# Fused attention and expert kernel: row parts earlier in the routing list, five loads of v in the opening, pieces no longer held behind a score tile

## The chip, the cores and the metric

The kernel runs on one core of one Trainium2 chip. The metric is the device time of one execution in microseconds (us): the median over several runs, lower is better. One further execution was recorded by the profiler; its rows are the ones read below. Times inside it count from the start of its span.

## The reference

```python
def _attn_ref(u, v, z):                      # batch 8, seq 2496, d_model 256, d_qk 64
    scores = (1.0 / S) * np.matmul(z, z.transpose(0, 2, 1))
    attn = np.maximum(scores, 0.0) ** 2
    return u * np.matmul(attn, v)

def _moe_ref(x, expert_emb, tau, w1, w2):    # x is the attention's output, 19968 tokens, 8 experts, F = 1024
    logits = normalised(x) @ normalised(expert_emb).T / tau
    expert_idx = np.argmax(logits, axis=1)
    gate_w = softmax(logits) at expert_idx
    out[mask of e] = gate_w * (np.maximum(x[mask] @ w1[e], 0.0) @ w2[e])
```

Each token goes to one expert; the row that is sent to it is the token's attention output.

## The kernel before, in words

**Attention.** The 8 batches are worked through one after the other. A batch b has 5 query groups g of 512 tokens (the last has 448), and a group has 20 steps q, one for each key tile s of 128 tokens. The loop over the 800 (b, g, q, s) makes one step at a time. A score tile exists once for two groups: for a key tile of the group itself or of a later group it is computed by `scores` (two matmuls, L259 and L260), brought to `a` by ScalarE (ReLU L263, square L264) and cut by VectorE in `parts` into a high half (L299) and a low half (L300), two float16 numbers whose sum is the value. They lie in a tile `hl`, of which there are five in turn. Where the key tile is of a later group, the tile is also turned by a DMA transpose on the SP queue (L313 into `tt`, L315 where half of it goes into the tile `joint`), so that the later group need not compute it: the first group of a batch, (b,0), has 16 such transposes, (b,1) fewer, (b,4) none. `scores` runs LOOK = 3 tiles ahead of use. `values` then multiplies the halves with the halves of v (L357, L359, L361) and sums over the 20 steps in the banks `acc`.

**Routing.** When a group's last step is done, `route` gives a list of small pieces, and one piece is popped in each step of the next group, behind `values`. In turn they are: `gate_x` (attention times u, L407), `fold` (for the last group only does it do anything), four `square` (L418, sums of squares on ScalarE), `root` (from L682), `scale` (L426 to L435, which makes `up`, the power of two that brings each row into range), four `split` (a block of 128 tokens each: the high half on ScalarE L441, the low half on VectorE L442, then a transpose of the row on the SP queue, L445, into `rowt`), `logits` (L453 on TensorE, from `rowt`), `norms` (L457 to L459, reads the logits from a bank of `acc` that the group after next will use), `top`, `exps` (L480), `gates`, `rank` (L497, L498 on TensorE), `place` (L507 to L515) and `scatters` (L521, on GpSimd). The route of (b,4) so runs during (b+1,0), and that of (b,0) during (b,1). The index in the list sets the step: piece 0 is popped at once at the end of the group, piece i behind step i-1 of the next group.

**Order of the instructions.** Each engine and each DMA queue works in order. The order is made by a scheduler from the program; `tc.issue_after(x)` keeps what is written under it behind the instruction x on the engine. In this kernel `state["at"]` is the newest ReLU of a score tile on ScalarE (L263), and `state["dv"]` the newest high half on VectorE (L299); every popped piece is issued under both.

**What shares the SP queue.** The loads of v for the next batch (L107, 256 KB each), the pieces of z for its largest value (`scan`, L114), u (L375), the experts' weights (L558, L561) and their stores (L621), and all the transposes, L313, L315 and L445.

**Opening.** z and v are scaled by powers of two that come from their largest absolute values. For batch 0 z is loaded in two pieces, one on the SP queue and one on ScalarE's, then v in ten loads of two key tiles that alternate between the two queues; `scan_max` (L121) reduces each of the twelve pieces on VectorE. ScalarE then splits z (L192, L194) with VectorE (L195, L199), and v (L223, with L224 on VectorE).

**Experts.** From about 1360 us on, TensorE multiplies the sorted rows with the experts' weights, to the end. The change does not touch this part.

## Time and profile before

| | us |
|---|---|
| median of 3 runs | 2193.96 (2192.53 to 2197.41) |
| the profiled execution | 2197.87 |
| its span | 2196.1 |
| busy TensorE (PE) | 2106.9, 96% of the span |
| busy VectorE (DVE) | 1333.8, 61% |
| busy ScalarE (ACT) | 1014.2, 46% |
| busy GpSimd (POOL) | 334.0, 15% |

The table gives each engine's busy time over the whole span, an average over the attention, where all engines work, and the experts, where TensorE works almost alone. The profile's strip of TensorE's granted clock shows 8 or 9 tenths of full speed in the first slice and 9 in all others, where 9 stands for anything from 90% up, so short stretches at half speed must be looked for by windows. In the strip of DMA activity the attention's slices stand at 6 to 9 tenths of the 16 DMA engines' time. An idle stretch of an engine counts only where a chain of waits to the end goes through it.

### The profile page before, as it was taken

To read this page: it belongs to the slowest core of one execution; us is meant where nothing else is said; L and a number is where in the kernel's file an instruction comes from. 1 tells how busy PE (TensorE), PEld (TensorE's weight loads), DVE (VectorE), ACT (ScalarE), POOL (GpSimd) and SP (SyncE) were. 2 spreads that over 40 slices of the span, in tenths; PEclk is the share of its full clock that TensorE was granted. 3 is DMA by queue.
4 is the path that set the end of the run, shared out by engine and by line. 5 is a ranking of instruction groups with operands and counts; after the bars stand their busy time and mean duration, and the time that the engine had idled before them with its cause. 6 is when DMAs were issued, how large, how long until landed. Compare 5 with 4: busy or idle time off the path is not lost.

```text
span 2196.1 us, 50747 instructions
## 1 busy us (share of the span) xinstructions
PE 2106.9 (96%) x19210; PEld 1794.6 (82%) x19210; DVE 1333.8 (61%) x4009; ACT 1014.2 (46%) x2131; POOL 334.0 (15%) x344
## 2 busy tenths in 40 slices
PE   5999899899899899999999999999999999999998
PEld 3788688688688688788788788888888888888888
DVE  7887777777787777787777765533333333333333
ACT  6666566566566566566566653222222222222211
POOL 0011022011011011011011011211211121111111
PEclk8999999999999999999999999999999999999999
DMA  6977977977967966976977787533333342247574
GB/s 172 176 145 170 198 142 171 194 141 166 201 140 163 206 141 153 205 153 152 201 156 154 146 162 181 132 88 88 72 75 88 88 89 58 50 109 201 133 211 115
DMA packets 661769, 317.61 MB, mean 145 GB/s; under 512 B 562949, under 2 KB 639246, under 8 KB 655376
## 3 DMA queue, kind: packets, MB, share of 16 engines
q1 hardware_dynamic: 644688, 271.39, 59.5%
q0 software_dynamic: 15184, 41.24, 6.2%
q8 instruction: 152, 2.49, 0.5%
q10 hardware_dynamic: 1648, 1.70, 0.3%
q14 instruction: 97, 0.79, 0.1%
HBM read 255.11 MB, written 59.60 MB: 143 GB/s over the span
## 4 chain that ended last, share of the span: by engine, by line
PE 83%; DMA 7%; DVE 6%; issue 1%; ACT 1%; SPq 1%; DVEq 0%; ACTq 0%; POOL 0%; POOLq 0%
PE acc L357 12%; PE acc L361 12%; PE acc L359 12%; PE po L974 6%; PE po L973 6%; PE po L975 6%; PE sc L259 4%; PE sc L260 3%; DMA rowt<-row 2%; PE acc L364 1%; PE acc L366 1%; PE pt L453 1%; DVE smxv L121 1%; DMA scan<-in_zT_dram 0%; DMA zt<-in_zT_dram 0%
## 5 line engine op out<-in xcount | busy, mean ns | idle before, releaser
L263 ACT ACTIVATE a<-sc 128x512 f32<-128x512 f32 (+1 forms) x480 | 270.6, 564 | 410.6 <-PE sc L260 347.6
L521 POOL DMA_INDIRECT xs<-row,dsti x160 | 173.7, 1086 | 1063.2 <-issue 286.9
L264 ACT ACTIVATE a<-a 128x512 f32<-128x512 f32 (+1 forms) x480 | 285.0, 594 | 7.8
L357 PE MATMUL acc<-vv,tt 128*128 128x256 f16 x1152 | 268.8, 272 | 0.0
L359 PE MATMUL acc<-vv,tt 128*128 128x256 f16 x1152 | 268.8, 272 | 0.0
L980 POOL DMA_INDIRECT out_dram<-ot,me x159 | 154.6, 972 | 660.0 <-DVE ot L979 626.9
L973 PE MATMUL po<-w,hh 128*128 128x256 f16 x928 | 253.0, 273 | 0.0
L974 PE MATMUL po<-w,hh 128*128 128x256 f16 x928 | 252.9, 273 | 0.0
L975 PE MATMUL po<-w,hl 128*128 128x256 f16 x928 | 252.9, 273 | 0.0
L979 DVE TENSOR_SCALAR ot<-po,me,w 128x256 f32<-128x256 f32 x116 | 58.3, 540 | 216.4 <-PE po L975 215.1
L259 PE MATMUL sc<-z 128*128 128x512 f16 (+1 forms) x480 | 178.7, 372 | 5.1 <-DVE z L199 3.5
L260 PE MATMUL sc<-z,z 128*128 128x512 f16 (+1 forms) x480 | 178.7, 372 | 0.0
L361 PE MATMUL acc<-vv,tt 128*128 128x256 f16 x1152 | 178.0, 273 | 0.0
L975 PEld LDWEIGHTS <-hl 128*128 128x128 f16 x1272 | 124.5, 98 | 14.4
L974 PEld LDWEIGHTS <-hh 128*128 128x128 f16 x1272 | 124.5, 98 | 14.3
L973 PEld LDWEIGHTS <-hh 128*128 128x128 f16 x1272 | 124.5, 98 | 14.2
L361 PEld LDWEIGHTS <-tt 128*128 128x128 f16 x1152 | 112.7, 98 | 13.0
L359 PEld LDWEIGHTS <-tt 128*128 128x128 f16 x1152 | 112.6, 98 | 12.8
L357 PEld LDWEIGHTS <-tt 128*128 128x128 f16 x1152 | 112.5, 98 | 12.8
L973 PE MATMUL po<-wb,hh 128*128 128x256 f16 x344 | 93.8, 273 | 0.0
L974 PE MATMUL po<-wb,hh 128*128 128x256 f16 x344 | 93.8, 273 | 0.0
L975 PE MATMUL po<-wb,hl 128*128 128x256 f16 x344 | 93.8, 273 | 0.0
(5238 smaller groups left out, 5504.2 us busy)
## 6 DMA issues: line engine op xcount, KB each, us to landing
w<-wsd SPq DMA_DIRECT2D x64, 1026.0 KB
wa<-wsd SPq DMA_DIRECT2D x46, 1024.0 KB
w<-wsd SPq DMA_DIRECT2D x42, 1024.0 KB
wb<-wsd SPq DMA_DIRECT2D x24, 1026.0 KB
vr<-in_v_dram SPq DMA_DIRECT2D x75, 256.0 KB
ut<-in_u_dram SPq DMA_DIRECT2D x72, 256.0 KB
wr<-in_w_dram SPq DMA_DIRECT2D x64, 256.0 KB
wsd<-wo SPq DMA_DIRECT2D x64, 256.0 KB
```

What stands on the lines that cost most here:

```text
L259: nc.tensor.matmul(sc[:, :n], z1[:, ss], z1[:, t0:t0 + n], start=True, stop=False)
L260: nc.tensor.matmul(sc[:, :n], z1[:, ss], z2[:, t0:t0 + n], start=False, stop=True)
L263: state["at"] = nc.scalar.activation(a[:, :n], sc[:, :n], AF.Relu, scale=2.0 ** -SHIFT).ins
L264: nc.scalar.activation(a[:, :n], a[:, :n], AF.Square)
L357: nc.tensor.matmul(outs[j], piece(ph, j), vh, start=first and j % 2 == 0, stop=False, skip_group_check=True)
L359: nc.tensor.matmul(outs[j], piece(ph, j), vl, start=False, stop=False, skip_group_check=True)
L361: nc.tensor.matmul(outs[j], piece(pl, j), vl if last else vh, start=False, stop=ends, skip_group_check=True)
L521: put = nc.gpsimd.indirect_dma_start(xs[:, :], bass.IndirectOffsetOnAxis(ap=loc["dsti"][:m, j:j + 1], axis=0), row[:m, j, :], None)
L973: nc.tensor.matmul(o, hh[:, f, t], wh, start=(f == 0), stop=False)
L974: nc.tensor.matmul(o, hh[:, f, t], wl, start=False, stop=False)
L975: nc.tensor.matmul(o, hl[:, f, t], wh, start=False, stop=(f == NF - 1))
L980: put = nc.gpsimd.indirect_dma_start(out, bass.IndirectOffsetOnAxis(ap=me.bitcast(U32)[:, j, 1:2], axis=0), ot[:, j, :], None, bounds_chec ...
```

## The change

Three edits.

1. In `route` the list is rearranged: `gate_x` moves from index 1 to 0, the four squares from one per step into two pairs (indices 2 and 3), `root` from 7 to 5, `scale` from 8 to 6, the splits from 9 to 12 to 7 to 10. The list is padded so that `logits` and all behind it stand one index later than before (18 instead of 17).
2. A popped piece is no longer held behind the newest score tile's instructions (`state["at"]`, `state["dv"]`).
3. In the opening z comes for its largest value in three pieces (512, 512 and 256 columns; SP, ACT, SP) in buffers of the ring of v, and v in five loads of four key tiles (512 KB), all on the SP queue, into buffers that the experts' weights use later (`v_first`). `scan_max` has 3 + 5 pieces instead of 2 + 10.

```diff
--- before.py
+++ after.py
@@ -116,7 +116,7 @@
 
     def scan_max(b, what, i):
         if i == 0:
-            n = NVP if what == "v" else ZSCANS if b else 2
+            n = (NVP if b else NV0) if what == "v" else ZSCANS if b else 3
             scan[b, what] = sml.tile([P, n], F32, name="smx" + what)
         nc.vector.tensor_reduce(scan[b, what][:, i:i + 1], scan.pop((b, what, i)), axis=AX.X, op=ALU.max,
                                 apply_absolute_value=True)
@@ -203,6 +203,26 @@
         c = slice(c0, c1)
         nc.sync.dma_start(z1[DQ:P, c], z2[0:DQ, c])
         nc.sync.dma_start(z2[DQ:P, c], z1[0:DQ, c])
+
+    VC = 4
+    NV0 = ceil_div(NST, VC)
+    v0 = []
+
+    def v_first(i):
+
+        if not v0:
+            assert NST * D <= 3 * min(W1, W2)
+            v0.extend([wp.tile([P, W1], F32, name="v0a", tag="wr1"), wp.tile([P, W2], F32, name="v0b", tag="wr2"),
+                       wp.tile([P, 2 * max(W1, W2)], F16, name="v0c", tag="wo").bitcast(F32)])
+        per = min(W1, W2) // D
+        assert per % VC == 0
+        q = i * VC
+        n = min(VC, NST - q)
+        t = v0[q // per][:, q % per * D:(q % per + n) * D].rearrange("p (j d) -> p j d", d=D)
+        nc.sync.dma_start(t, v[0, q * P:(q + n) * P, :].rearrange("(j p) d -> p j d", p=P))
+        for j in range(n):
+            vraw[0, q + j] = t[:, j, :]
+        scan[0, "v", i] = t.rearrange("p j d -> p (j d)")
 
     def v_split(b, s):
         vt = vraw.pop((b, s))
@@ -539,9 +559,9 @@
         assert nj == 4
         none = lambda: None
         one = lambda f, *a: lambda: f(*a)
-        begin = [none, gate_x, none, both(fold, one(square, 0)), one(square, 1), one(square, 2), one(square, 3), root, scale]
-        begin += [one(split, j) for j in range(nj)]
-        begin += [none] * (NST - 3 - len(begin))
+        two = lambda j: both(one(square, j), one(square, j + 1))
+        begin = [gate_x, none, both(fold, two(0)), two(2), none, root, scale] + [one(split, j) for j in range(nj)]
+        begin += [none] * (NST - 2 - len(begin))
         return begin + [logits, norms, top, exps, gates, none, none, rank, none, place, scatters]
 
 
@@ -639,21 +659,22 @@
     nc.vector.memset(ones_f, 1.0)
     first = tc.manual_schedule(engines={mybir.EngineType.DVE, mybir.EngineType.Activation})
     first.__enter__()
-    z0 = wp.tile([P, W1], F32, name="z0", tag="wr1")
-    for i in range(2):
-        t = z0[:, 2 * i * SCAN:2 * (i + 1) * SCAN]
-        src = zT[0, i * (DQ // 2):(i + 1) * (DQ // 2), :]
-        (nc.scalar if i % 2 else nc.sync).dma_start(t, src.rearrange("a c -> (a c)").rearrange("(p w) -> p w", p=P))
-        scan[0, "z", i] = t
+    zw = SP * DQ // P
+    zsrc = zT[0, 0:DQ, :].rearrange("a c -> (a c)").rearrange("(p w) -> p w", p=P)
+    for i in range(3):
+        c = slice(512 * i, min(512 * (i + 1), zw))
+        zs = vring.tile([P, 2, D], F32, name="zs", tag="vv").rearrange("p j d -> p (j d)")[:, :c.stop - c.start]
+        (nc.scalar if i == 1 else nc.sync).dma_start(zs, zsrc[:, c])
+        scan[0, "z", i] = zs
     nc.scalar.dma_start(idt, ident)
     z_tiles(0)
     ZN = ceil_div(SP, ZC)
     for k in range(2):
         z_load(0, k * ZC)
-    for i in range(NVP):
-        scan_load(0, "v", i, nc.scalar if i % 2 else nc.sync)
+    for i in range(NV0):
+        v_first(i)
     z_load(0, 2 * ZC)
-    for i in range(2):
+    for i in range(3):
         scan_max(0, "z", i)
     for f in scale_pieces(0, "z"):
         f()
@@ -664,9 +685,9 @@
     halves = {}
     for i in range(LOOK + 1):
         probs[direct[i]] = scores(*direct[i])
-    for i in range(NVP):
+    for i in range(NV0):
         scan_max(0, "v", i)
-        if i == NVP - 3:
+        if i == NV0 - 2:
             halves[direct[0]] = parts(*direct[0], probs.pop(direct[0]))
     z_load(0, 3 * ZC)
     for f in scale_pieces(0, "v"):
@@ -1110,8 +1131,7 @@
                     todo.pop(0)[2]()
         values(accs[b, g], b, g, q, s, *half(b, g, s))
         if queue:
-            with tc.issue_after(state["at"]), tc.issue_after(state["dv"]):
-                queue.pop(0)()
+            queue.pop(0)()
         if i >= wnext and not state["pm"]:
             wnext += wgap
             if wq:
```

Lines of the program behind `v_first` stand 20 further down in the changed kernel: L313 becomes L333, L445 becomes L465, and so on.

What the order of the instructions becomes, at three places.

**The SP queue in the middle of group (2,0)**, where the route of (1,4) runs. `tt<-hl` are the transposes of score tiles, `rowt` those of the row blocks, `vr`, `wsd`, `wr1`, `scan` plain loads and stores. Before:

```order
L107 DMA vr_5785<-in_v_dram 128x2x256
L621 DMA wsd_73<-wo_5348 128x2x512
L313 DMA_TRANSPOSE tt_5806<-hl__5803 128x8x128
L445 DMA_TRANSPOSE rowt_5801<-row1_100 128x4x128
L313 DMA_TRANSPOSE tt_5806<-hl__5829 128x8x128
L445 DMA_TRANSPOSE rowt_5801<-row1_100 128x4x128
L313 DMA_TRANSPOSE tt_5806<-hl__5854 128x8x128
L445 DMA_TRANSPOSE rowt_5801<-row1_100 128x4x128
L107 DMA vr_5865<-in_v_dram 128x2x256
L558 DMA wr1_5882<-in_w1_dram 128x512
L445 DMA_TRANSPOSE rowt_5801<-row1_100 128x4x128
L313 DMA_TRANSPOSE tt_5806<-hl__5885 128x8x128
```

and now:

```order
L333 DMA_TRANSPOSE tt_5667<-hl__5769 128x8x128
L107 DMA vr_5779<-in_v_dram 128x2x256
L641 DMA wsd_73<-wo_5335 128x2x512
L465 DMA_TRANSPOSE rowt_5738<-row1_100 128x4x128
L333 DMA_TRANSPOSE tt_5799<-hl__5796 128x8x128
L465 DMA_TRANSPOSE rowt_5738<-row1_100 128x4x128
L333 DMA_TRANSPOSE tt_5799<-hl__5822 128x8x128
L333 DMA_TRANSPOSE tt_5799<-hl__5844 128x8x128
L107 DMA vr_5855<-in_v_dram 128x2x256
L578 DMA wr1_5869<-in_w1_dram 128x512
L333 DMA_TRANSPOSE tt_5799<-hl__5872 128x8x128
L114 DMA scan_5882<-in_zT_dram 128x320
```

The score tile of `hl__5854` before is that of `hl__5844` now (and `hl__5885` that of `hl__5872`). Of the four row transposes two now stand above the rows shown, so all four are ahead of that tile's transpose, where two were; the plain loads keep their place beside the score transposes.

**ScalarE early in group (2,1)**, where the route of (2,0) runs. `a<-sc` (ReLU) and `a<-a` (square) are the two instructions of a score tile, `sq` the squares of the routing, `row` its splits, and `ex` the exponentials of the route before. Before:

```order
L263 ACTIVATE a_6190<-sc_6187 128x512
L418 ACTIVATE sq_6212,n2_6102<-x_6100 128x256
L264 ACTIVATE a_6190<-a_6190 128x512
L263 ACTIVATE a_6222<-sc_6219 128x512
L418 ACTIVATE sq_6241,n2_6102<-x_6100 128x256
L264 ACTIVATE a_6222<-a_6222 128x512
L263 ACTIVATE a_6252<-sc_6249 128x512
L264 ACTIVATE a_6252<-a_6252 128x512
L263 ACTIVATE a_6303<-sc_6300 128x512
L264 ACTIVATE a_6303<-a_6303 128x512
L263 ACTIVATE a_6336<-sc_6333 128x512
L441 ACTIVATE row0_99<-x_6100,up_6321 128x256
```

and now:

```order
L500 ACTIVATE ex_6088<-sh_6077 128x32
L283 ACTIVATE a_6060<-sc_6057 128x512
L284 ACTIVATE a_6060<-a_6060 128x512
L438 ACTIVATE sq_6132,n2_6087<-x_6085 128x256
L438 ACTIVATE sq_6134,n2_6087<-x_6085 128x256
L438 ACTIVATE sq_6152,n2_6087<-x_6085 128x256
L438 ACTIVATE sq_6154,n2_6087<-x_6085 128x256
L461 ACTIVATE row0_99<-x_6085,up_6254 128x256 x4
L283 ACTIVATE a_6181<-sc_6178 128x512
L284 ACTIVATE a_6181<-a_6181 128x512
```

The four squares and the four splits stand together ahead of one score tile; before, the last two squares and the four splits stood between the tiles, at most one for each.

**ScalarE in the opening**, up to its first score tile. Before:

```order
L646 DMA z_110<-in_zT_dram 128x640
L648 DMA idt<-in_ident_dram 128x128
L107 DMA vr<-in_v_dram 128x2x256 x5
L192 ACT_TABLE_LOAD
L192 ACTIVATE z_114<-zt,scz 64x256
L194 ACTIVATE z_115<-zt,scz 64x256
L192 ACTIVATE z_114<-zt,scz 64x256
L194 ACTIVATE z_115<-zt,scz 64x256
L192 ACTIVATE z_114<-zt,scz 64x256
L194 ACTIVATE z_115<-zt,scz 64x256
L263 ACTIVATE a<-sc 128x512
```

and now:

```order
L667 DMA zs<-in_zT_dram 128x512
L669 DMA idt<-in_ident_dram 128x128
L192 ACT_TABLE_LOAD
L192 ACTIVATE z_117<-zt,scz 64x256
L194 ACTIVATE z_118<-zt,scz 64x256
L192 ACTIVATE z_117<-zt,scz 64x256
L194 ACTIVATE z_118<-zt,scz 64x256
L283 ACTIVATE a<-sc 128x512
L284 ACTIVATE a<-a 128x512
```

The five loads of v are gone from ScalarE's queue ahead of the table load, and the first score tile stands ahead of the third pair of z's splits.

## Rows read from the trace of the kernel before

**Rows 1.** Waits of PE over the whole span: total us, times, longest us.

```profile
PE pt L453 <- DMA rowt<-row: 48.2, 22, 3.8
```

**Rows 2.** Stretches: us, busy of each engine, granted PE clock, DMA share, GB/s.

```profile
160.00:1120.00 960.00, 913.36 (x8014) 748.05 (x8012) 728.43 (x2451) 582.79 (x1285) 131.73 (x127) 0.98 0.82 170
365.00:406.00 41.00, 35.88 (x296) 28.07 (x295) 28.72 (x84) 23.34 (x50) 4.14 (x4) 0.92 1.00 211
```

**Rows 3.** Timeline of PE in group (2,0): start, us, engine, operation, idle before.

```profile
387.99 0.35 PE L453 MATMUL pt<-e,rowt 128*128 128x16 f16 x8
391.11 0.28 PE L453 MATMUL pt<-e,rowt 128*128 128x16 f16 x4 [2.77 <-DMA rowt<-row]
393.59 0.27 PE L453 MATMUL pt<-e,rowt 128*128 128x16 f16 x4 [2.21 <-DMA rowt<-row]
...
394.52 1.06 PE L357 MATMUL acc<-vv,hl__5980 128*128 128x256 f16 x4
...
397.08 0.42 PE L357 MATMUL acc<-vv,joint 128*128 128x256 f16 x1
```

**Rows 4.** Timeline of the SP queue in groups (2,0) and (2,1).

```profile
366.85 1.27 SPq L313 DMA_TRANSPOSE tt<-hl__5622  x1
...
384.13 1.23 SPq L445 DMA_TRANSPOSE rowt<-row  x1
385.45 1.27 SPq L313 DMA_TRANSPOSE tt<-hl__5854  x1
...
393.03 0.58 SPq L114 DMA_DIRECT2D scan<-in_zT_dram  x1
...
407.45 1.23 SPq L313 DMA_TRANSPOSE tt<-hl__6214  x1
```

**Rows 5.** Timeline of DVE in group (2,0).

```profile
380.60 0.48 DVE L442 SCALAR_TENSOR_TENSOR row<-x,up,row 128x256 f16<-128x256 f32 x1
...
388.85 0.43 DVE L299 CAST hl__5980<-a 128x512 f16<-128x512 f32 x1 [1.51 <-DMA tt<-hl__5854]
...
395.85 0.49 DVE L121 TENSOR_REDUCE smxz<-scan 128x1 f32<-128x320 f32 x1 [5.63 <-DMA scan<-in_zT_dram]
396.25 0.42 DVE L300 TENSOR_TENSOR joint<-a,joint 128x256 f16<-128x256 f32 x1
```

**Rows 6.** Timeline of all engines in group (2,1), tile by tile.

```profile
403.55 0.42 ACT L418 ACTIVATE sq<-x 128x256 bf16<-128x256 f32 x1 [2.96 <-DVE x L407]
...
407.99 0.43 DVE L299 CAST hl__6245<-a 128x512 f16<-128x512 f32 x1
...
411.47 0.27 PE L357 MATMUL acc<-vv,hl__6245 128*128 128x256 f16 x1
...
413.91 0.50 ACT L441 ACTIVATE row<-x,up 128x256 f16<-128x256 f32 x1
...
425.85 1.30 SPq L313 DMA_TRANSPOSE tt<-hl__6411  x1
...
429.29 0.43 DVE L299 CAST hl__6529<-a 128x512 f16<-128x512 f32 x1 [3.33 <-DMA tt<-hl__6411]
...
431.28 0.26 PE L453 MATMUL pt<-e,rowt 128*128 128x16 f16 x4 [2.80 <-DMA rowt<-row]
...
431.82 1.02 PE L357 MATMUL acc<-vv,hl__6529 128*128 128x256 f16 x4
```

**Rows 7.** Timeline of ACT, DVE and PE in the opening.

```profile
8.11 1.28 ACT L192 ACT_TABLE_LOAD   x1 [8.11 <-DMA vr<-in_v_dram]
...
14.70 0.51 ACT L192 ACTIVATE z<-zt,scz 64x256 f16<-64x256 f32 x1 [3.20 <-DMA zt<-in_zT_dram]
...
18.41 0.43 DVE L299 CAST hl__201<-a 128x512 f16<-128x512 f32 x1 [1.52 <-ACT a L264]
...
21.56 0.16 DVE L132 TENSOR_REDUCE smv<-smxv 128x1 f32<-128x10 f32 x1
...
25.81 0.37 PE L357 MATMUL acc<-vv,hl__201 128*128 128x256 f16 x1 [0.97 <-ACT vv L223]
```

## The prediction

> **What bounds the kernel now.** I read the waits of TensorE (PE) first, then the granted clock by windows, then the timelines around the largest wait, then the opening. One wait stands far above the rest: the routing's logits (L453) wait for the transposed row blocks `rowt`, 48.2 us in 22 waits, none over 3.8 [rows 1]. They lie in 15 groups: the eight (b,1), which host the route of (b,0), and the seven (b,0) from b = 1 on, which host that of (b-1,4). The clock shows a second loss: over the 960 us of the attention's middle the mean granted clock is 0.98, so about 2% or 19 us of full speed is missing at most, and in the 41 us of group (2,0) it is 0.92, so 3.3 us [rows 2]; of TensorE's two levels, 1.2 and 2.4 GHz, this is the lower one for some 6.6 us, behind waits of together 5.0 us [rows 3].
>
> Why are the blocks late? The low half of the last block was made on VectorE at 380.60 [rows 5], but PE got the last `rowt` only at 393.59 [rows 3]. Between lies the SP queue. In (2,0) it is without a real gap from 366.85 to the transposes and loads that end shortly before 407.45, each transpose holding it 1.23 to 1.27 us, and two blocks stand behind score transposes and loads [rows 4]. The DMA engines' share in that window is 1.00 [rows 2]. So the group is bound by what this one queue issues, and PE feels it at the logits first. A second thing is just as tight: the ring of five `hl` tiles. VectorE's high half at 388.85 had waited 1.51 us for the score transpose issued at 385.45 [rows 4, 5], and in (2,1) the one at 429.29 waited 3.33 for that of 425.85, while PE wanted this very tile at 431.82, right behind the logits' wait of 2.80 [rows 6].
>
> **The change part by part.** I go by the profiled execution, 2197.87, which stands 3.9 above the median of 2193.96.
>
> *Row parts sooner, in (b,0).* The four row transposes are ahead of the score transpose of 385.45 now, where two were. Nothing is taken off the queue: 2 x 1.25 = 2.5 us go from the row blocks' lateness to the score transpose's. So the high half of 388.85 comes at about 391.4 and is done at 391.8, and PE waits there instead, from 387.99 plus its work until 391.8. Its products started at 394.52 before [rows 3]: 2.7 us are won so far, because the logits now follow behind this step and find their blocks there. The next step gives some back. Its low half (396.25) stands on VectorE behind the reduce of `scan`, whose DMA the queue issues at 393.03, behind all four row transposes both before and now, and which was ready at 395.85 [rows 4, 5]. So that half is still done at 396.25 + 0.42 = 396.7. The low product is the third kind in a step and comes some 1.2 us after its first, so the step can begin at 395.5 to 395.8 instead of 397.08 [rows 3]: 1.3 us won. Bounds: nothing, if the score transposes lose all that the blocks win, and 5.0 (2.77 + 2.21), if the scan lands sooner. I take 1.3, the value of the row nearest to it, in seven groups: 9.1 us.
>
> *Row parts sooner, in (b,1).* PE would reach the products of 431.82 at 429.0 without its 2.80. One more row transpose is now ahead of the score transpose of 425.85, so the tile's high half moves from 429.29 to 430.5 and is done at 430.95 [rows 6]: 0.9 won at most by this chain, 2.8 if the queue gets ahead earlier in the group, nothing if it does not. Half of 0.9, since the bunch below costs this group something: 0.4 x 8 = 3.2 us.
>
> *Pieces no longer behind a score tile.* In the (b,1) groups four squares and four splits now stand together on ScalarE ahead of one tile's ReLU: 4 x 0.42 + 4 x 0.50 = 3.7 us, of which two squares stood ahead of it before, so 2.8 more; the read of each square's sum adds a little [rows 6]. What covers it: that tile's high half was at 407.99, and PE's first product of it at 411.47, 3.5 us later [rows 6]; and squares and splits begin one to two steps sooner. Between squares and splits ScalarE now also waits for VectorE's `up`, behind a reduce of 0.49 and a pair of halves of 0.43 and about 0.7 [rows 5], some 2 us. Cost 0 to 1.4 us for each group. I take 0 beyond what the line above holds back. On VectorE the four low halves of 0.48 move the same way, under the same cover. The SP queue may then stand idle while its next row transpose waits for its block; that cover is the loads already in flight.
>
> *Later pieces.* Logits, norms, rank and place stand one step later. The logits read blocks long there. The norms must be read out before the group after next writes the same bank; behind the last step there is little left, at most one high half of 0.43 [rows 5] could stand ahead, so 0 to 0.4 in some groups, taken as 0. The scatters on POOL have nobody waiting within the attention.
>
> *Opening.* ScalarE's table load stood behind five issues of v until 8.11; with them gone, the first split can follow z's scale at once, some 0.4 sooner than 8.11 + 1.28 [rows 7]. The first score tile no longer stands behind the split that waited until 14.70. VectorE's first high half at 18.41 had waited 1.52 for it, and behind this half stood the last reduces of v and `smv` at 21.56, from which v's scale and the first product of 25.81 follow [rows 7]. So about 1.5 come through. The reduces read the same elements in 5 pieces instead of 10, and v's bytes are the same on one queue instead of two. Bounds 0 (v lands later on one queue) and 4; I take 2.0. No row of before shows v loaded so, hence the 0. The Trainium skill's page "DMA: Bandwidth & Descriptors", section "Issuing engines are not separate DMA queues", says that a DMA runs on the same 16 engines whoever issues it and that a second issuer saves only issue time; by it alone v would land as before, and the lower bound would be the 2.0 and not 0.
>
> *Sum.* 2197.87 - 2.0 - 9.1 - 3.2 = 2183.6, less the 3.9: **2180 us**. The clock I leave as it is: PE still waits about as long once in these groups, at another place.
>
> **The rivals.**
>
> *All waits go* (chance 0.10). The queue gets ahead, because blocks issued sooner take idle time at the group's start, and the `hl` ring never bites. Then 48.2 and the clock's 19 both come back: 2197.87 - 2.0 - 67.2 - 3.9 = 2125. For it: the queue has idle time before 407.45. Against it: it has none from 366.85 to there [rows 4], and the ring's waits of 1.51 and 3.33 are already there [rows 5, 6].
>
> *The wait changes its name only* (0.17). Every block moved ahead holds a score transpose back as long, the ring of five stops VectorE, and PE waits as long for `hl`. Only the opening is won: 2197.87 - 2.0 - 3.9 = 2192. For it speaks the queue without gaps; against it, that PE waits twice in (2,0), at 391.11 and 393.59, and the second wait is for a block that now has nothing left ahead of it. The Trainium skill's page "Perfetto Trace Analysis", sections "What 'DMA-bound' means" and "DMA Optimizations", has this as a rule: where the issuing engine's track is solid with DMA slices, the issue itself is the limit, and larger DMAs or a second issuer help. The change does neither in the groups. The trace agrees as far as the solid track goes [rows 4].
>
> *The bunch stalls PE, slower* (0.13). If ScalarE's 2.8 us and its wait for `up` of about 2 come on top of each other and the sooner start does not pay for it, tile and PE are late by 2.8 + 2.0 - 3.5 = 1.3 in each of 8 groups: 10.4, and with the clock behind it, at 3.3 for 5.0 us of waiting, 17. The SP queue starves meanwhile, so nothing is won at the group's end: 2197.87 - 2.0 + 17 - 3.9 = 2209. It decides from where the tile's high half is over 3.5 us later than now. The slack is as large as the price, hence no small chance.
>
> **How the numbers follow.** The forecast, a part of the wait won, has 0.60, with a range of its own from 2152 (opening 4, 2.0 in each (b,0) and 1.9 in each (b,1), and 3.3 for 5.0 of the clock with it: 4 + 29 x 1.66 = 52, little short of which I stop) to 2192. Taking in the change of name, the range is **2150 to 2196**; the two far rivals stay outside, some 2 in 10. A measurement here can tell about 0.2%, 4.4 us, from no change, so faster means under 2189.6. Faster: 0.54 of the forecast's, all 0.10, and 0.03 of the change of name, 0.67. Same: 0.05 of the forecast's, 0.12 of the change of name, 0.01 of the bunch's, 0.18. Slower: 0.15.
>
> **What the changed profile would show.** Right: PE's wait for `rowt` falls from 48.2 to under 15, a new wait for score tiles (VectorE's L319, PE's L357 or L259) of 20 to 35 us takes the place, VectorE's waits for `tt` grow, and the SP queue in (b,0) stays without gaps; the clock over the attention's middle stays near 0.98; the first product of values comes some 2 us before 25.81. Wrong: a clock of 1.00 there and no new waits (all go), a sum of waits as before (the name only), or new PE waits a third of the way into (b,1), with gaps on the SP queue behind them (the bunch).

## The result and the profile after

The changed kernel takes 2171.22 us, the median of 5 runs (2163.75 to 2171.68), beside 2196.97 for the kernel before (5 runs, 2192.53 to 2199.58): ratio of the runs 0.9864, 95% interval 0.9843 to 0.9885 (the quotient of the two medians is 0.9883). A second measurement gave 0.9838 (0.9821 to 0.9854). The forecast was 2180, with a range of 2150 to 2196.

The first profile of the changed kernel is of its fastest execution (2163.75, span 2162.0); a second one took 2170.80 (span 2169.0), close to the median. Timelines are shown from the first; where measured terms are held against the forecast at the end, they are the second's unless said otherwise. A group's time is counted from its first product of values to that of the next group.

| us, changed minus before | first profile | second profile | forecast |
|---|---|---|---|
| first product of values (25.81 before) | -3.3 | -3.4 | -2.0 |
| the eight groups (b,0) | -16.3 | -14.8 | -9.1 |
| the eight groups (b,1) | -10.8 | -11.8 | -3.2 |
| groups (b,2) to (b,4) | -1.8 | +0.7 | 0 |
| behind the attention | -1.9 | +2.1 | 0 |
| span | -34.1 | -27.1 | -14.3 |

PE's waits over the whole span, where [rows 1] had 48.2 us for `rowt` and now no wait for it is left; us in total, times, longest:

```profile
PE acc L381 <- DVE joint L320: 4.1, 3, 2.1
...
PE acc L377 <- DVE hl__6491 L319: 1.9, 1, 1.9
...
PE acc L377 <- DVE hl__3864 L319: 1.7, 1, 1.7
...
PE acc L377 <- DVE lg L478: 1.5, 3, 0.8
```

Beside these stand some twenty waits for one tile `hl` each, 0.4 to 1.6 us, and a few shorter ones; all waits for `hl` together make 22.3 us. So much of the lost time did not vanish, it moved to the score tiles, in shorter pieces: PE's idle time within the groups, added up from the timeline, falls from 58.7 to 38.4, and to 39.9 in the second profile. The windows (us, busy of PE, PEld, DVE, ACT and POOL, granted clock, DMA share, GB/s), to be held against [rows 2]:

```profile
160.00:1120.00 960.00, 928.23 (x8220) 753.54 (x8218) 734.49 (x2519) 610.88 (x1332) 137.72 (x129) 1.00 0.83 174
357.00:397.00 40.00, 35.22 (x290) 26.86 (x288) 27.58 (x80) 22.10 (x45) 4.21 (x4) 0.96 1.10 223
```

The clock of the middle is 1.00 to two digits instead of 0.98, and 0.96 instead of 0.92 in (2,0). PE's busy time over the whole span, for the same 19210 matmuls, is 2098.6 instead of 2106.9: 8.3 of the first profile's 34.1 us are busy time and the other 25.8 idle time; in the second profile PE is busy 2101.6, 5.3 less than before. That matmuls which no longer run at the lower level make the 8.3 is likely, but not shown by itself: the kernel with the smaller ring of v below has 1.00 over the middle too and is busy 2105.4.

Group (2,0) on PE, for [rows 3]; the group begins at 349.32, where it began at 358.28 before, so 9.0 is to be added for a comparison:

```profile
378.14 0.28 PE L377 MATMUL acc<-vv,hl__5919 128*128 128x256 f16 x1 [1.62 <-DVE hl__5919 L319]
...
380.81 0.28 PE L377 MATMUL acc<-vv,hl__5945 128*128 128x256 f16 x1 [0.65 <-DVE hl__5945 L319]
...
382.56 0.60 PE L377 MATMUL acc<-vv,hl__5967 128*128 128x256 f16 x4
...
383.43 0.55 PE L473 MATMUL pt<-e,rowt 128*128 128x16 f16 x16
...
384.27 0.27 PE L377 MATMUL acc<-vv,joint 128*128 128x256 f16 x1
...
388.81 0.42 PE L377 MATMUL acc<-vv,joint 128*128 128x256 f16 x1
```

The logits (L473, all 16 matmuls) run without a wait. In front of them PE now waits twice for a high half, 1.62 and 0.65. The SP queue there and VectorE, for [rows 4, 5]:

```profile
372.91 1.27 SPq L465 DMA_TRANSPOSE rowt<-row  x1
...
375.59 1.27 SPq L465 DMA_TRANSPOSE rowt<-row  x1
...
378.31 1.29 SPq L333 DMA_TRANSPOSE tt<-hl__5844  x1
...
382.13 0.58 SPq L114 DMA_DIRECT2D scan<-in_zT_dram  x1
...
394.12 0.57 SPq L107 DMA_DIRECT2D vr<-in_v_dram  x1
```

```profile
377.65 0.43 DVE L319 CAST hl__5919<-a 128x512 f16<-128x512 f32 x1 [2.56 <-DMA tt<-hl__5796]
...
386.79 0.48 DVE L121 TENSOR_REDUCE smxz<-scan 128x1 f32<-128x320 f32 x1 [3.88 <-DMA scan<-in_zT_dram]
387.19 0.41 DVE L320 TENSOR_TENSOR joint<-a,joint 128x256 f16<-128x256 f32 x1
```

The row transposes of 372.91 and 375.59 are the last two of four, and the score transpose of 378.31, the one of 385.45 before, comes 1.8 us later counted from the group's start. VectorE's high half at 377.65 waited 2.56 for an earlier one, where the worst wait of this group was 1.75 before. The reduce of `scan` still holds back the low half of the joint tile (387.19): its load stands at 382.13, behind all of them.

Group (2,1), begun at 391.31 (400.45 before, so 9.1 to be added), SP queue, VectorE and PE, for [rows 6]:

```profile
399.48 5.63 SPq L465 DMA_TRANSPOSE rowt<-row  x4
405.20 1.29 SPq L333 DMA_TRANSPOSE tt<-hl__6264  x1
...
413.33 1.23 SPq L333 DMA_TRANSPOSE tt<-hl__6377  x1
...
415.28 1.23 SPq L333 DMA_TRANSPOSE tt<-hl__6401  x1
```

```profile
419.35 0.43 DVE L319 CAST hl__6491<-a 128x512 f16<-128x512 f32 x1 [3.39 <-DMA tt<-hl__6377]
...
421.48 0.42 DVE L319 CAST hl__6516<-a 128x512 f16<-128x512 f32 x1
```

```profile
419.83 0.28 PE L377 MATMUL acc<-vv,hl__6491 128*128 128x256 f16 x1 [1.91 <-DVE hl__6491 L319]
...
421.95 0.61 PE L377 MATMUL acc<-vv,hl__6516 128*128 128x256 f16 x4
...
423.13 0.55 PE L473 MATMUL pt<-e,rowt 128*128 128x16 f16 x16
```

The four row transposes go out together from 399.48 on, 5.63 us for the four, ahead of all but one of the score transposes. `hl__6516` is the tile that PE wanted at 431.82 before, and 415.28 the score transpose that was issued at 425.85. Its high half comes at 421.48, 430.6 on the old scale, and PE's products of it start at 421.95, 431.1 on the old scale, 0.7 sooner. The wait now stands one step ahead of it: 1.91 for a high half that waits 3.39 for the score transpose of 413.33; the 2.80 for `rowt` are gone. The opening, for [rows 7]:

```profile
12.31 0.60 ACT L283 ACTIVATE a<-sc 128x512 f32<-128x512 f32 x1 [1.62 <-PE sc L280]
...
15.76 0.41 DVE L319 CAST hl__189<-a 128x512 f16<-128x512 f32 x1
...
18.84 0.16 DVE L132 TENSOR_REDUCE smv<-smxv 128x1 f32<-128x5 f32 x1
...
22.47 0.37 PE L377 MATMUL acc<-vv,hl__189 128*128 128x256 f16 x1 [0.98 <-ACT vv L243]
```

The first score tile comes at 12.31 instead of 15.75, the first high half at 15.76 instead of 18.41, `smv` at 18.84 instead of 21.56, the first product at 22.47 instead of 25.81.

### The profile page after: what moved, and what is told of

Read it like the earlier page. It is cut to its first block, busy times and chain, and to the rows that moved or that the text cites. A ratio compares the mean times of both kernels' runs of the same rounds, so it can differ in the third digit from the quotient of the medians.

```text
span 2162.0 us, 50660 instructions
## 1 busy us (share of the span) xinstructions
PE 2098.6 (97%) x19210; PEld 1779.8 (82%) x19210; DVE 1312.5 (61%) x4005; ACT 1025.6 (47%) x2131; POOL 343.8 (16%) x344
## 5 line engine op out<-in xcount | busy, mean ns | idle before, releaser
L541 POOL DMA_INDIRECT xs<-row,dsti x160 | 183.5, 1147 | 1097.1 <-issue 243.1
L284 ACT ACTIVATE a<-a 128x512 f32<-128x512 f32 (+1 forms) x480 | 286.3, 596 | 11.9
L994 PEld LDWEIGHTS <-hh 128*128 128x128 f16 x1272 | 124.4, 98 | 14.3
```

The lines of the kernel that those rows point to most:

```text
L284: nc.scalar.activation(a[:, :n], a[:, :n], AF.Square)
L541: put = nc.gpsimd.indirect_dma_start(xs[:, :], bass.IndirectOffsetOnAxis(ap=loc["dsti"][:m, j:j + 1], axis=0), row[:m, j, :], None)
L994: nc.tensor.matmul(o, hh[:, f, t], wh, start=(f == 0), stop=False)
```

## The experiments

Theory P, later Q: the SP queue bounds (b,0) and (b,1); PE feels it through `rowt` or through the ring of `hl`, and what comes first on the queue decides which. Ratios are to runs of the kernel before on the same chip, with 95% intervals; changes of groups, in us, are profile against profile of the kernel before. Such a profile is one execution; those of the two kernels with v from GpSimd from batch 2 on and nothing else new are of their fastest (2137.46 and 2177.37), so their groups look somewhat better than a median run.

| kernel | median us | ratio | (b,0) | (b,1) | (b,2) to (b,4) |
|---|---|---|---|---|---|
| opening alone | 2199.28 | 0.9976 (0.9964 to 0.9988) | -2.1 | -0.2 | +3.6 |
| opening and list | 2192.90 | 0.9946 (0.9926 to 0.9965) | -10.5 | +7.9 | -1.0 |
| opening and release | 2189.48 | 0.9924 (0.9905 to 0.9943) | -11.9 | -8.1 | +10.6 |
| the changed kernel again | 2169.46 | 0.9838 (0.9821 to 0.9854) | -14.8 | -11.8 | +0.7 |
| six hl tiles, smaller ring of v | 2182.20 | 0.9929 (0.9910 to 0.9949) | -13.2 | -19.5 | +19.7 |
| smaller ring of v alone | 2187.84 | 0.9941 (0.9922 to 0.9960) | -14.9 | -10.5 | +20.9 |
| row transposes twice | 2275.51 | 1.0352 (1.0331 to 1.0373) | +23.2 | +19.9 | +17.6 |
| v from GpSimd | 2150.13 | 0.9777 (0.9760 to 0.9794) | -29.2 | -22.8 | -1.6 |
| v from ScalarE | 2164.19 | 0.9832 (0.9811 to 0.9853) | -18.3 | -9.6 | -1.8 |
| v from GpSimd from batch 2 on | 2145.87 | 0.9755 (0.9739 to 0.9772) | -30.8 | -23.6 | -0.9 |
| the same and z's scan | 2134.68 | 0.9704 (0.9688 to 0.9720) | -32.7 | -27.8 | -2.1 |
| before, v from GpSimd from batch 2 on | 2181.38 | 0.9922 (0.9903 to 0.9941) | -19.2 | -11.6 | +11.3 |

**The parts of the change.** Opening alone: the changed kernel with these two places as before.

```diff
-        two = lambda j: both(one(square, j), one(square, j + 1))
-        begin = [gate_x, none, both(fold, two(0)), two(2), none, root, scale] + [one(split, j) for j in range(nj)]
-        begin += [none] * (NST - 2 - len(begin))
+        begin = [none, gate_x, none, both(fold, one(square, 0)), one(square, 1), one(square, 2), one(square, 3), root, scale]
+        begin += [one(split, j) for j in range(nj)]
+        begin += [none] * (NST - 3 - len(begin))
...
-            queue.pop(0)()
+            with tc.issue_after(state["at"]), tc.issue_after(state["dv"]):
+                queue.pop(0)()
```

> The changed kernel with the old list of pieces and with pieces held behind score tiles again: of the change only the opening is left; the row transposes stand on the SP queue exactly where they stood before. Theory P (the place of the row transposes on the SP queue makes the gain in the groups): gain only in the opening, the first product of values 3.3 us sooner than 25.81, PE's wait for rowt stays near 48, the clock of the middle near 0.98; ratio 0.997 to 1.000, about 2191. Rival O (a large part comes from the opening, by a shift of everything that follows against the queue): ratio below 0.994, rowt's wait clearly under 40.

PE's waits:

```profile
PE pt L473 <- DMA rowt<-row: 43.6, 21, 3.5
```

As theory P had it: `rowt` waits as before, and the gain, 0.24%, is the opening's.

Opening and list: only the second hunk of that diff.

> The changed kernel with pieces held behind score tiles again: opening and the new list. On the SP queue the row transposes now stand 2 to 3 score transposes ahead of their old place in (b,0) and 2 to 4 in (b,1), where the changed kernel has them 3 to 8 ahead. Theory P: about half of what the changed kernel wins in the groups: rowt's wait falls from 48 to 10 to 25, clock 0.99, ratio 0.991 to 0.995, about 2182. Rival L (the list makes it all): ratio 0.986 to 0.989 as the changed kernel, rowt's wait near 0. Rival U (the release from the tiles makes it all): ratio as with the opening alone, 0.997 to 1.000.

```profile
PE pm L597 <- DVE mx L595: 4.1, 1, 4.1
...
PE acc L377 <- DVE hl__9120 L319: 3.5, 1, 3.5
PE acc L377 <- DVE hl__11748 L319: 3.3, 1, 3.3
...
PE acc L377 <- DVE hl__6491 L319: 2.6, 1, 2.6
```

The theory was half right. No wait for `rowt` is left at all, with the row transposes only half as far ahead; but PE waits for `hl` instead, up to 3.5 us at once, (b,1) loses 7.9, and the list adds 0.30% to the opening's 0.24%. This is the rival "the wait changes its name", in (b,1). Of the 7.9, 5.6 are (5,1), where PE waits 4.1 for the largest value of an expert's weights (L595); that reduce stands on VectorE behind a high half that had waited 3.40 for a score transpose.

Opening and release: only the first hunk.

> The changed kernel with the old list of pieces: opening and pieces no longer held. On the SP queue the four row transposes of (b,1) stand where the changed kernel has them, in (b,0) two of the four do and two stand where they stood before. Theory P: (b,1) wins as in the changed kernel (some 1.3 us for each of the eight), (b,0) only a little, since the last two blocks still come late; and the logits stand one step earlier than in the changed kernel: rowt's wait 10 to 20, ratio 0.990 to 0.994, about 2180. Rival U: ratio 0.986 to 0.989. Rival L: 0.997 to 1.000.

```profile
PE pt L473 <- DMA rowt<-row: 7.2, 3, 2.8
...
PE pm L134 <- DVE pos L532: 5.2, 4, 1.8
```

The release alone adds 0.52%. It brings (b,1) most of what it wins in the changed kernel, -8.1 of -11.8, and leaves 7.2 us of `rowt`. A cost shows that nobody expected: with the old list `place` stands one step earlier, in (b,2) beside the piece that takes the largest value of the next batch's z across the partitions, and this piece (L134) waits for the one bank that `place` (L532) still reads, 5.2 us; (b,2) is 8.1 us longer. With the new list and the release together, as in the changed kernel, no such wait is left.

The changed kernel again:

> The changed kernel itself, beside the three parts on the same chip: ratio 0.984 to 0.989 by every theory, no wait for rowt, clock 0.99 to 1.00. It gives a second profile, which tells how much of the profiled 34 us is this execution's own (the runs shown lie at 2168 to 2172, the profiled one at 2163.75).

```profile
160.00:1120.00 960.00, 926.54 (x8211) 751.80 (x8210) 732.40 (x2517) 607.55 (x1333) 133.37 (x127) 1.00 0.82 174
```

List and release together bring 1.38% beyond the opening, where the two apart bring 0.82%. The row transposes go furthest ahead only with both. With both PE no longer waits for `rowt` or the bank, and no wait for `hl` is over 1.9 in the first profile and 2.8 in the second, where the list alone has 3.5.

**The ring of hl.** `bufs=6` for `hl`, paid for by the ring of v:

```diff
-    vring = actx.enter_context(tc.tile_pool(name="vring", bufs=2 * NVP + 2))
+    vring = actx.enter_context(tc.tile_pool(name="vring", bufs=2 * NVP + 1))
...
-            hl = wk.tile([P, GT, 2, P], F16, name="hl_", tag="hl", bufs=5)
+            hl = wk.tile([P, GT, 2, P], F16, name="hl_", tag="hl", bufs=6)
...
-            hl = wk.tile([P, 2, 512], F16, name="hl_", tag="hl", bufs=5)
+            hl = wk.tile([P, 2, 512], F16, name="hl_", tag="hl", bufs=6)
```

> The changed kernel with a ring of six hl tiles instead of five; the room (2 KB per partition) comes from the ring of v, 21 buffers instead of 22. Theory Q (what is left in (b,0) and (b,1) is the SP queue, felt through the ring of hl): the high halves get 1.25 to 2 us more room behind the score transposes, PE's waits for hl (some 15 to 20 us together) fall under 6, the waits for the joint tile's low half, which hang on the scan's DMA behind the same queue, stay at 3 to 5; ratio to before 0.975 to 0.981, about 10 us under the changed kernel. Rival S (the ring is no limit of its own, the queue's lateness comes out elsewhere: scan, joint, rowt): PE's waits move to those and the ratio stays at 0.982 to 0.986. Rival V (the ring of v becomes the limit): slower than the changed kernel, with waits behind v's loads.

And the control, with the first hunk alone:

> The changed kernel with 21 instead of 22 buffers in the ring of v and five hl tiles, the control for the ring of six. If the 19 us that (b,3) lost there come from v's ring (Rival V), they stay here, (b,1) is as in the changed kernel, and the ratio is 0.992 to 0.998. If they came from the sixth hl tile, this kernel is as the changed one, 0.982 to 0.986.

PE's waits with six tiles:

```profile
PE acc L381 <- DVE joint L320: 11.9, 5, 3.5
```

and in the control:

```profile
PE acc L381 <- DVE joint L320: 3.9, 3, 2.2
...
PE acc L377 <- DVE hl__12749 L319: 2.8, 1, 2.8
```

The price is v's ring: the control loses 20.9 in (b,2) to (b,4) and (b,3), where v's halves for the next batch begin to be made, is 22.8 longer than in the first profile of the changed kernel, one tile's wait there alone 2.8 (`hl__12749`). The kernel with six tiles pays nearly the same, 19.0. Against the control, the sixth tile wins 9.0 in (b,1) and nothing in (b,0) (+1.7). The two times cannot be told apart (0.9929 and 0.9941, with intervals that overlap), so this rests on the two profiles. By them the ring itself is a limit in (b,1). In (b,0) it is not: there the lateness comes out as the wait for the joint tile's low half, 11.9 us in place of 3.9, behind the scan's load on the same queue, for which VectorE waits 54.0 us in all where the control has 19.0. That is rival S for (b,0) and theory Q's own case for (b,1).

**The queue's length.** Each row transpose issued twice:

```diff
             nc.sync.dma_start_transpose(loc["rt"][:, j, :, :], row16[:, j, 0:2 * D])
+            nc.sync.dma_start_transpose(loc["rt"][:, j, :, :], row16[:, j, 0:2 * D])
```

> The changed kernel with each row transpose issued twice, to the same place: 4 more transposes of some 1.25 us on the SP queue for each group, 5 us. Theory Q: (b,0) and (b,1) have no room on the queue, so each loses 3 to 5 us (45 to 75 us over 15 of them, and the clock's half speed comes back in part), while (b,2) to (b,4), whose queue has idle time, stay within 0.5 us; ratio to before 1.005 to 1.02. Rival T (the row transposes only had to come sooner; the queue's length is no limit): ratio 0.983 to 0.990, all groups as in the changed kernel.

```profile
PE ph__21670 L971 <- DMA wa<-wsd: 10.7, 1, 10.7
PE acc L381 <- DVE joint L320: 9.9, 5, 3.5
PE pt L474 <- DMA rowt<-row: 8.9, 10, 2.6
```

Against the changed kernel's first profile (b,0) loses 39.5 and (b,1) 30.7, 4.4 for each of the 16 groups, where 5 us went onto the queue; (b,2) and (b,3) lose 5.2 together in 16 groups. In the groups that the theory names nearly every microsecond added to the SP queue is one of the kernel; but the same transposes are also work added for the DMA engines, so this run does not tell the queue from the engines. The total is worse than expected: (b,4) loses 14.3, of it 12.0 in (5,4) and (6,4), where PE now waits for `rowt` (2.3 and 4.7). The part behind the attention loses some 16, of which 10.7 are one wait of PE for experts' weights (`wa`, L971), which are loaded by the SP queue too.

**Who issues.** The loads of v on GpSimd's queue instead of SP's:

```diff
-            (eng or nc.sync).dma_start(t, v[b, 2 * i * P:2 * (i + 1) * P, :].rearrange("(j p) d -> p j d", p=P))
+            (eng or nc.gpsimd).dma_start(t, v[b, 2 * i * P:2 * (i + 1) * P, :].rearrange("(j p) d -> p j d", p=P))
```

> The changed kernel with the loads of v for later batches issued by GpSimd instead of SP: the same bytes on the same 16 DMA engines, but about five issues of 0.57 us less on the SP queue in each of (b,0) and (b,1), 2.9 us. Theory Q: the remaining waits of PE for hl and joint fall by half or more, 0.5 to 2 us in each of the 15 groups; ratio to before 0.976 to 0.981. Rival D (the DMA engines themselves are full, their share is 1.0 or above in (2,0), so it does not matter who issues): ratio 0.983 to 0.986. A third way: GpSimd's own transfers (scatters of rows) stand behind the loads, and the ratio is worse than 0.986.

GpSimd in the opening and, for the ten loads of batch 3's v, in (1,3) and (1,4), which begins at 327.51; VectorE in the opening:

```profile
3.09 4.54 POOL L107 DMA_DIRECT2D vr<-in_v_dram  x6
...
313.70 1.53 POOL L107 DMA_DIRECT2D vr<-in_v_dram  x2
330.37 0.72 POOL L107 DMA_DIRECT2D vr<-in_v_dram  x1 [14.78 <-PE acc L386]
...
347.31 0.71 POOL L107 DMA_DIRECT2D vr<-in_v_dram  x1 [1.70 <-PE acc L386]
...
19.77 2.50 DVE L121 TENSOR_REDUCE smxv<-v0b 128x1 f32<-128x1024 f32 x2 [5.40 <-DMA v0b<-in_v_dram]
```

(b,0) and (b,1) win 25 us more than in the changed kernel. But the edit changes more than who issues. The SP queue reaches the loads of batch 3's v in (2,0) and (2,1) (one of them is the row at 394.12 above); GpSimd issues them as soon as their buffers are free, two in (1,3) and eight in (1,4). So not only the issues have left (b,0) and (b,1) but also the bytes. The windows of (2,0) and (2,1) together, in the changed kernel, with v from GpSimd and with v from ScalarE (the next run):

```profile
349.32:427.01 77.69, 70.74 (x587) 54.12 (x586) 58.57 (x174) 49.38 (x101) 8.19 (x8) 0.98 1.05 210
353.72:426.87 73.15, 68.64 (x587) 53.64 (x586) 58.59 (x174) 49.43 (x101) 8.26 (x8) 1.00 0.98 187
350.65:426.70 76.05, 69.82 (x587) 53.15 (x586) 58.98 (x174) 48.59 (x101) 8.67 (x8) 1.00 1.08 214
```

That is 16.3, 13.7 and 16.3 MB (GB/s times us). Theory Q's time came, but rival D, that the DMA engines are full in these groups, is not ruled out by it. 8 us went back in the opening: GpSimd had nothing before it, sent batch 1's v out from 3.09 on, and batch 0's own v came late, VectorE's reduce of `v0b` at 19.77 after a wait of 5.40. With ScalarE as the issuer (`nc.scalar` in the same place):

> The same five issues for each of (b,0) and (b,1) on ScalarE's queue instead of SP's. Theory Q: the SP queue gains as with GpSimd, but ScalarE stands still for each issue, 0.5 to 1.3 us, between score tiles; ratio 0.977 to 0.985. Rival D: 0.983 to 0.986 or, with ScalarE late for the score tiles, above.

```profile
ACT a L284 <- DMA rowt<-row: 22.2, 7, 6.1
```

Here the loads stay in (b,0) and (b,1). Against the second profile of the changed kernel, (b,0) wins 3.5 more and (b,1) 2.2 less, and the time is the changed kernel's, 0.9832 against 0.9838: ten issues less for each batch on the SP queue won nothing that shows. ScalarE is no free queue: its squares stood 22.2 us in seven waits, each behind a load of v that itself had to wait to be issued (the view puts the end of these waits down to the landing of a row transpose). So the run lies in the range of both, theory Q and rival D, and does not decide. Another number speaks for D. Added up from the timelines over the twelve groups (b,0) and (b,1) of batches 1 to 6, the SP queue made 381 issues in the changed kernel and was busy 395.1 us; here it made 321 and was busy 384.5, because each took longer; in the next run, where the bytes of v have left these groups too, the same 321 took 364.9.

With `nc.gpsimd if b > 1 else nc.sync` the early loads go:

> As the kernel with v from GpSimd, but the loads of batch 1's v are on the SP queue again: there GpSimd, with nothing before it, had moved ten loads into the opening, where they delayed batch 0's own v by 8 us. Theory Q and this reading of the opening: the first product of values back at 22.4 us, groups (b,0) and (b,1) with b from 1 or 2 on as with v from GpSimd; 6 to 8 us below it, ratio 0.973 to 0.976. Rival: the early loads had helped (0,0) to (1,1) as much as they cost in the opening, then 0.976 to 0.980.

```profile
160.00:1120.00 960.00, 947.99 (x8476) 778.56 (x8475) 753.98 (x2590) 628.55 (x1373) 180.22 (x190) 1.00 0.85 179
```

As expected: the first product is back at 22.3, the groups keep their gain (the loads of v stand in (b-1,3) and (b-1,4) again), and PE is busy 947.99 of the same 960 us, where the changed kernel had 928.23 and the kernel before 913.36. Then `scan_load` of z in the same way:

> As v from GpSimd from batch 2 on, with the four loads of z's scan for each of those batches on GpSimd too. In the changed kernel the last step of (b,0) waits for the joint tile's low half behind the reduce of a scan piece whose load stands late on the SP queue. Theory Q: these waits, 2 us in some groups, go, and the queue is shorter by 0.5 us for each piece: ratio 0.971 to 0.975, PE's wait for joint under 1 us. Rival: those loads wait for their one buffer on GpSimd and hold v's loads and the scatters behind them: no faster than with v alone.

```profile
160.00:1120.00 960.00, 951.77 (x8535) 786.76 (x8533) 758.22 (x2609) 631.62 (x1377) 199.09 (x217) 1.00 0.86 180
```

PE's wait for the joint tile is gone from the list of its waits, and 2134.68 us beats both kernels: 0.9704 of the kernel before, a little under the range. Here the loads that change their issuer stay in (b,0) and (b,1), and these groups move the same 78.9 MB in the six batches as in the run above; so for the scan's loads it is the issuing queue that cost time, by its order or by its length. Last, the kernel before with nothing but v on GpSimd from batch 2 on:

> The kernel before, with the loads of v from batch 2 on issued by GpSimd, and nothing of the change. Theory Q: the SP queue bounds (b,0) and (b,1) here too, so the row transposes come some 3 us sooner in the groups concerned, rowt's wait falls from 48 to 15 to 30, the clock of the middle rises to 0.99; ratio 0.988 to 0.993. Rival P2 (only the order on the queue matters): rowt's wait above 40, ratio 0.997 to 1.001.

```profile
PE pt L453 <- DMA rowt<-row: 37.5, 21, 3.8
```

The expectation was right on the time and wrong on the wait. `rowt` still costs 37.5, so the wait by itself was a poor measure; but (b,0) and (b,1) win 30.8 us, as much as with the changed kernel's own reordering (27.1 and 26.6 in its two profiles) or a little more. A part, 11.7, is lost again in (b,4), where PE now waits for `rowt` too, 0.7 to 2.1 in each of the first six, (0,4) to (5,4). These are the groups into which GpSimd brings eight of the ten loads of v; that the loads are in the way of the transposes there is likely, but no run tests it by itself.

## Why the prediction was right, and where it was off

**The mechanism was right in what the change does.** The order on the SP queue decides what PE waits for: with the row transposes where they were, `rowt` keeps 43.6 us (the opening alone); with them ahead, the blocks' lateness passes to the score transposes and the ring of `hl` (the list alone: `rowt` to 0, `hl` up to 3.5), and `scan` gives some of it back. What makes the queue late is open. The prediction says the group is bound by what this one queue issues, and notes beside it a share of the DMA engines of 1.00. Row transposes twice (4.4 us lost for 5 us added) and v from GpSimd change the issues and the bytes of these groups together; v from ScalarE, which changes the issues alone, won nothing, but ScalarE paid for it. Even the single steps of (2,0) came: the last tile's products start 33.2 us after the group's first instead of 36.2, so 3.0 sooner where 2.7 was worked out; the group's last step, which starts right behind the held one, 39.5 instead of 40.9, 1.4 sooner where 1.3 was forecast. And the sum of the profile: the wait for `rowt` under 15, new waits of 20 to 35 us (22.3 for `hl` and 4.1 for `joint`). One sign that it had named did not come: the clock of the middle did not stay near 0.98.

**Three terms were too small, and one was met on the average only.** Measured terms are the second profile's, the steps of (2,0) and (2,1) the first's.

*The clock, "I leave as it is":* by the granted clock it came back nearly whole, and PE's busy time, in which it shows, fell by 5.3 us in all (8.3 in the first profile). The argument was that PE waits about as long once, at another place. In (2,0) that is so: 4.8 us idle instead of 5.1. Over all groups it is not: 38.4 and 39.9 us in the two profiles instead of 58.7, and in shorter pieces, the longest behind the first group 2.1 and 2.8 instead of 3.8. Behind those the clock falls more seldom: 0.98 before, 1.00 in both profiles of the changed kernel. The list alone, whose waits go up to 4.1, has 0.99 in the same window; the kernel with the smaller ring of v, with 56.2 us idle in all but no wait over 2.8 behind the first group, has 1.00.

*(b,1), 0.4 for each group:* measured 1.5 (11.8 in 8), of which 9.1 are PE's idle time and 2.7 its busy time. In (2,1) the chain itself came out as worked: the high half at 430.6 on the old scale where 430.5 was forecast, PE's products 0.7 sooner where 0.9 was the bound. But half of that bound had been taken off for the bunch, which cost nothing there, and the two steps behind the wait, 2.52 and 2.2 us before, take 2.0 and 1.7 now, which is the clock again: 1.7 us for the group. And (2,1), from which the term was read, is not typical: PE's idle time fell by 0.7 there, but by 1.6, 2.7 and 1.8 in (0,1), (4,1) and (7,1). That is above the 0.9 of this chain and within the other bound, "2.8 if the queue gets ahead earlier in the group"; whether the queue got ahead there was not looked at.

*(b,0), 1.3 for each of seven groups:* measured 16.3 in these seven, 2.3 for each, of which 9.5 are idle time and 6.7 busy time; (0,0) is 1.5 longer. So the waits came to the 9.1 of the forecast, and what lies above it is busy time, which the sum had at nothing with the clock. But the agreement is one of the average: in (2,0), the group that was worked through, idle time fell by 0.4, in the other six by 0.1 to 2.2, and that they add up to 9.5 is in part luck. In (2,0) the clock did not help in the first profile: its last step, 1.3 us before, took 2.5 at the lower level and ate what had been won, so that the group is 0.2 shorter; in the second profile it took 1.8 and the group is 1.9 shorter.

**Smaller terms.** *Later pieces*, taken as 0: PE now waits for `lg`, the norms, 1.5 us in the first profile and 1.8 in the second, none over 0.8, and did not before. *The low end of the range* does not follow from its terms: 52 us from 2193.96 give 2142, ten below the 2152 stated. The result does not lie there, so nothing hangs on it.

**The opening** gave 3.3 and 3.4 instead of 2.0, by the chain forecast: first score tile, high half, reduces, `smv`.

**The rivals.** "All waits go" fell: 38.4 us of idle time stand in the groups. Its price was too high as well, for it counted 48.2 of idle and 19 of clock apart, though part of the half-speed time is waiting; busy time fell by 8.3 and 5.3. "The wait changes its name only" is what the list alone does in (b,1), but not the whole change. The Trainium skill's page "Perfetto Trace Analysis", sections "What 'DMA-bound' means" and "DMA Optimizations", which stood beside it, says that spreading the issues over the engines may help where the issue is the limit. The runs leave open whether that is the case here. ScalarE as the second issuer won nothing (0.9832 against 0.9838); GpSimd won 0.8 percentage points with v and 1.3 with z's scan too (0.9704), but the loads of v had then also moved to other groups. "The bunch stalls PE" fell. ScalarE does wait for `up`:

```profile
ACT row L461 <- DVE up L449: 32.2, 22, 3.8
```

1.5 us each, near the 2 assumed, but the sooner start pays for it. PE lost nothing behind it in (2,1) of the first profile, and 1.2 us in two waits where it was looked for, in (5,1) of the second.

## What to carry to other kernels

Where a queue is solid with issues for a whole group, moving work within it shifts the wait to whoever is now behind, and wins what the idle stretches at its ends can take. To win more, work has to leave the group; when a load gets another issuer, look at when it then starts and not only at whose queue it leaves, since a queue with little before it runs ahead: here into two groups with room, which helped, and into the opening, which cost 8 us. Read a term from several groups before multiplying it by eight: the one group that was worked through gave 0.4 us of idle time where others gave up to 2.2. Price a wait with the slow clock behind it, and expect several short waits to cost less than a few long ones of about the same sum.

## What was not expected of the hardware

A queue that is solid with issues need not be the limit by itself. With ScalarE as the issuer the SP queue had 60 issues less in twelve groups, and its busy time fell by 10.6 us, 0.18 for each, where such an issue had held it 0.57 (the median); the bytes were the same and the DMA engines' share of (2,0) and (2,1) 1.08. With GpSimd the bytes went too, into groups such as (1,4), where the share rose from 0.57 to 0.89, and the kernel won 25 to 28 us more in (b,0) and (b,1) than the changed kernel. How much of that is issue and how much is bytes stays open: a run that leaves the bytes in the groups and lets nobody wait for the issuer is missing. GpSimd took some 0.75 us for an issue (six in 4.54), and its busy time grew by 56 us over the run with z's scan too (398.2 against 342.2), none of which PE waited for.
